# Late expert slots of an attention and mixture-of-experts kernel: rows gathered in quarters and turned on VectorE instead of TensorE

## The chip, the cores and the metric

One core of one Trainium2 chip runs the whole program. The metric is the device time of one execution in microseconds (us); for several executions it is their median. PE is TensorE's matmul, PEld its weight load, DVE is VectorE, ACT is ScalarE, POOL is GpSimd, SP is SyncE.

## The reference

The first half is an attention through 32 memory slots per head (8 batches, 8 heads, 576 rows, head width 64); its result, 4608 tokens of 512 numbers, is the input `x` of a mixture of 8 experts. Each token goes to the one expert with the largest logit:

```python
logits = x @ w_gate
e_idx = np.argmax(logits, axis=1)
...
for e in range(E):
    mask = e_idx == e
    h = np.maximum(x[mask] @ w1[e], 0.0)     # 512 -> 1024
    ye = h @ w2[e]                           # 1024 -> 512
    out[mask] = gate_w[mask, None] * eom[mask, e, None] * ye
```

The weights and the matmuls are float32. The kernel splits each operand into a rounded part and a rest (`xh`, `xl`; the two halves of `whl`; `hh`, `hl`) and adds three products.

## The kernel before

**Slots.** The experts' work is cut into slots of 3, 2 or 1 blocks of 128 tokens; all blocks of a slot belong to one expert, which is known only at run time. Slots 0 to 4 (three blocks each, index tables "a" and "b") are filled while attention still runs. Slots 5 to 9 (three blocks) and 10 to 13 (two blocks) are listed by the last table, "l", once all tokens are routed. Slots 14 and up hold one block each, stand behind branches and are not entered with these inputs, so the program works through 14 slots with 38 blocks.

**One slot** (`several`, L1111 to L1154). Its first layer takes four weight chunks of 128x1024 (u = 0 to 3) and runs 96 matmuls at L1127, weights standing, tokens moving; `hh` and `hl` come out of PSUM through ACT (L1132) and DVE (L1133). The second layer takes four chunks more (u = 4 to 7). For each chunk it goes through the slot's blocks k, and for each block it runs 6 matmuls at L1146 into the block's PSUM bank `py[k]`. One such group of 6 is a step: 12 steps in a slot of three blocks, 8 in one of two. Behind the last chunk of a block `finish_y` scales the block on ACT (L1106) and scatters its rows to `out` with an indirect DMA from POOL (L1107). Consecutive scatters write the same tensor, and each waits for the landing of the one before.

**Input of the next slot.** `gather` (L479 to L486) issues one indirect DMA on POOL per block, which brings one row of 576 floats per partition into `xg`; a row is four quarters of 144 floats, each 128 columns of `x` and 16 of gate numbers. The hook in the work loop issues the gathers of slot i+2 during slot i, behind the last scatter of slot i-1. At four fixed steps of slot i's second layer (`TURN`, `nxt`) `turn_x` (L978 to L995) turns the next slot's `xg`: TensorE transposes 128x128 squares against `ident` into a PSUM bank (L993), ACT copies the bank rounded to `xh` (L994), DVE subtracts that from the bank to `xl` (L995). Slots of three blocks do 3 transposes at each of the four steps; slots of two do 4 transposes at two of them. That is 4 transposes per block, 152 in all.

**Weights.** `Stream` fetches chunks from `wall` (512 KB each, SP queue), ACT casts (L521) and DVE subtracts (L522), up to 9 chunks ahead of use in a ring of 10.

**Index tables.** `table` (L205 to L242) builds an index list by 36 matmuls (L227), reads them from PSUM on DVE (L233 to L242) and writes `idx_g` for the gathers and `idx_o` for the scatters.

Of the kernel before, what the change touches and what calls it, by code (L numbers as in the profile page):

```python
# [16 lines left out]
P = 128  # L17
# [48 lines left out]
def attention_moe(tc, phiT, kv, qT, wgo, wall, out):  # L66
# [3 lines left out]
    with contextlib.ExitStack() as ctx:  # L70
# [20 lines left out]

        idx = {}
        for nm, n in (("a", 3 * NPS[0]), ("b", 3 * NPS[1]), ("l", NBL)):
            idx[nm] = (cp.tile([P, n], I32, name="idx_g" + nm), cp.tile([P, n], I32, name="idx_o" + nm))
# [46 lines left out]
        V.tensor_copy(tok_hl[:, 0], tok_j[:])  # L141
        V.tensor_scalar(tok_j[:], tiv, 63, None, ALU.bitwise_and)
        V.tensor_copy(tok_hl[:, 1], tok_j[:])
        su.__exit__(None, None, None)

        upto = cp.tile([P, E, E], F32, name="upto")
# [58 lines left out]
        def table(nm, q, nch, nblk):  # L205

            while nm == "l" and "rl" not in env:
                yield
            bw = (env["rl"] if nm == "l" else rt).tile([P, nch, 2, nblk], BF16, name="bw" + nm)
            w = min(nch, 9 * NBL // nblk // 9 * 9)  # L210
            for c in range(0, nch, w):
                b3 = [P, w, nblk]
                eq = rt.tile([P, 9 * NBL], BF16, name="eq")
                eq = eq[:, 0:w * nblk].rearrange("p (c b) -> p c b", c=w)
                V.tensor_tensor(eq, iota_blk[:, 0:nblk].unsqueeze(1).to_broadcast(b3),
                                q[:, c:c + w].unsqueeze(2).to_broadcast(b3), ALU.is_equal)
                yield
                for i in range(2):
                    V.tensor_tensor(bw[:, c:c + w, i], eq,
                                    tok_hl[:, i, c:c + w].unsqueeze(2).to_broadcast(b3), ALU.mult)  # L220
                yield
            yield
            yield from take_pr()
            yield from hold(LATE["pe"])
            pi = ps_r.tile([P, 2, NBL], F32, name="pr")
            for c in range(nch):
                T.matmul(pi[:, :, 0:nblk], Aw[:, c], bw[:, c], start=(c == 0), stop=(c == nch - 1))  # L227
            yield
            yield from hold(LATE["dve"])
            iv = rt.tile([P, NBL], F32, name="iv")  # L230
            i2 = rt.tile([P, NBL], F32, name="i2")
            ivv, i2v = iv[:, 0:nblk], i2[:, 0:nblk]
            V.tensor_copy(i2v, pi[:, 1, 0:nblk])  # L233
            yield
            V.scalar_tensor_tensor(ivv, pi[:, 0, 0:nblk], 64.0, i2v, ALU.mult, ALU.add)
            taken.clear()
            yield
            ig, io = idx[nm]
# [3 lines left out]
            V.scalar_tensor_tensor(io[:], ivv, -1.0, i2v, ALU.add, ALU.add)  # L242

        def counts(bp):
            pr = ps_r.tile([P, NCH, E], F32, name="pr")
# [60 lines left out]
        def route_late():  # L306
# [159 lines left out]
        for s in range(NSLOT):  # L466
            nb = 3 if s < NPE + NPT else 2 if s < NPE + NPT + NPP else 1
            if s < NPE:
                k = s >= NPS[0]
                nm, q0, rows = "ab"[k], 3 * (s - NPS[0] * k), (k + 2) * NCH * P  # L470
            else:
                j = s - NPE
                q0 = 3 * j if nb == 3 else NB3 + 2 * (j - NPT) if nb == 2 else NB3 + NB2 + j - NPT - NPP
                nm, rows = "l", NTOK
            slots.append({"s": s, "nb": nb, "q0": q0, "idx": idx[nm], "rows": rows,
                          "known": False, "listed": False})
        order = slots

        def gather(z):  # L479
            z["xg"] = xgs.tile()  # L480
            for k in range(z["nb"]):
                q = z["q0"] + k
                G.indirect_dma_start(  # L483
                    out=z["xg"][:, k], out_offset=None, in_=xs[0:z["rows"]],
                    in_offset=bass.IndirectOffsetOnAxis(ap=z["idx"][0][:, q:q + 1], axis=0),
                    bounds_check=z["rows"] - 1, oob_is_err=False)  # L486

        def known(*zs):
            for z in zs:
                z["known"] = True  # L490

        class Stream:
# [485 lines left out]
        def turn_x(z, c):  # L978


            nb, xg = z["nb"], z["xg"]
            if c == 0:
                z["x"] = (mo.tile([P, 4, 3 * P], F32R, name="xh"), mo.tile([P, 4, 3 * P], F32R, name="xl"))
            xh, xl = z["x"]
            n = nb * P
            w = 1 if nb == 3 else 2
            if c % w:
                return
            pt = bank([w, 512 // w], "ps")
            for j in range(w):  # L990
                for k in range(nb):
                    o = (c + j) * XQ
                    T.transpose(pt[:, j, k * P:(k + 1) * P], xg[:, k, o:o + P], ident[:])  # L993
            A.copy(xh[:, c:c + w, 0:n], pt[:, :, 0:n])  # L994
            V.tensor_tensor(xl[:, c:c + w, 0:n], pt[:, :, 0:n], xh[:, c:c + w, 0:n].bitcast(F32), ALU.subtract)  # L995

        NT = 5 * NBP
        deferred = []
# [104 lines left out]

        def finish_y(z, k, py):
            y = mo.tile([P, DM], F32, name="y", bufs=2)
            A.activation(y[:], py, AF.Copy, scale=z["xg"][:, k, P:P + 1])  # L1106
            G.indirect_dma_start(  # L1107
                out=out, out_offset=bass.IndirectOffsetOnAxis(ap=z["idx"][1][:, z["q0"] + k:z["q0"] + k + 1], axis=0),
                in_=y[:], in_offset=None, bounds_check=NTOK - 1, oob_is_err=False)

        def several(i, st, nxt, hook):  # L1111
# [29 lines left out]
            for u in range(4, 8):  # L1141
                w = st.take(i, u)
                for k in range(nb):
                    for f in range(2):
                        for n, (a, b) in enumerate(PASS):
                            T.matmul(py[k], h[u - 4][a][:, f, k * P:(k + 1) * P], w[:, b, DM * f:DM * f + DM],  # L1146
                                     start=(u == 4 and f == 0 and n == 0), stop=(u == 7 and f == 1 and n == 2))
                    if u == 7:
                        finish_y(z, k, py[k])
                    hook()  # L1150
                    step = nb * (u - 4) + k
                    if step in TURN[nb]:
                        nxt(TURN[nb].index(step))
                st.done(PUMP[0])  # L1154

        def single(i, st, nxt):
            z = order[i]
# [48 lines left out]
        def settle():  # L1206

            att.finish()
            pso.close()
            pa.close()  # L1210
            env["hs"] = ctx.enter_context(tc.tile_pool(name="hs", bufs=1, side="right", reuse_waits="tile"))
            env["rl"] = ctx.enter_context(tc.tile_pool(name="rl", bufs=1, side="right", reuse_waits="tile"))
            grow(1)
            env["ps"] = ctx.enter_context(tc.tile_pool(name="p1", bufs=7 - NPK, space=PSUM, reuse_waits="tile"))

# [49 lines left out]
def _layout(inputs):  # L1265
# [19 lines left out]
    wall = np.concatenate([w1, w2], axis=2)  # L1285
    return [("phiT", phiT), ("kv", kv), ("qT", qT), ("wgo", wgo), ("wall", wall)]


# [16 lines left out]
```

## Time and profile before

| | |
|---|---|
| median of 3 runs | 595.18 us (593.45 to 597.05) |
| the profiled execution, its own time | 595.97 us |
| span from first to last instruction in it | 594.3 us |
| PE busy | 539.3 us, 91% of the span |
| DVE, ACT, POOL busy | 340.9, 273.0, 160.7 us |
| matmuls | 4107 |

A row of the instruction timeline gives start and duration in us, the engine, line, operation and tiles, how many instructions are merged into it (x3), and in brackets how long the engine was idle before and who released it. Matmuls are pipelined: a matmul's duration overlaps the next ones, so what one costs is read from the distance between starts.

### The profile page before, as it was taken

Reading aid. Unit: us, or ns where it says so; the run is one execution under the profiler, and the core shown is the slowest. Engines: PE = TensorE matmul, PEld = TensorE weight load, DVE = VectorE, ACT = ScalarE, POOL = GpSimd, SP = SyncE. Lnnn points to the kernel's source line nnn. Section 1 sums busy time; section 2 is a strip of 40 time slices with the busy share of each in tenths; the row PEclk is TensorE's granted clock in tenths of the full one; section 3 lists DMA queues with packets and bytes.
Section 4 is the critical chain, followed back from the end, with each engine's and each line's share of the span. In section 5 each row is a group of like instructions: output and inputs, shape, how many; then the busy total and the mean of one; then the engine's idle time right before and its main releaser. Section 6 shows DMA issues by size and latency. Waiting matters only on the chain. (4 is left out here: it accounts for less than half of the span.)

```text
span 594.3 us, 10781 instructions
## 1 busy us (share of the span) xinstructions
PE 539.3 (91%) x4107; PEld 464.3 (78%) x4107; DVE 340.9 (57%) x686; ACT 273.0 (46%) x456; POOL 160.7 (27%) x192
## 2 busy tenths in 40 slices
PE   3788677788999999999999999999999999999980
PEld 2455455487788898998989899898989988989970
DVE  4487789677855589983544535354453526556200
ACT  4376554544445365434435444444444445555310
POOL 2244376731345036203303030130303012300100
PEclk9979879879999999999999999999999999999995
DMA  8999999974558578646646446474645538762000
GB/s 300 413 374 387 410 378 324 318 251 142 160 169 299 174 243 281 213 128 200 219 142 206 130 162 192 136 221 142 199 126 166 164 136 261 242 206 82 28 18 13
DMA packets 41276, 124.13 MB, mean 209 GB/s; under 512 B 9408, under 2 KB 9472, under 8 KB 40832
## 3 DMA queue, kind: packets, MB, share of 16 engines
q1 hardware_dynamic: 35136, 102.71, 52.2%
q0 software_dynamic: 6080, 20.65, 9.7%
q8 instruction: 34, 0.56, 0.4%
q14 instruction: 26, 0.21, 0.1%
HBM read 102.99 MB, written 20.87 MB: 208 GB/s over the span
## 5 line engine op out<-in xcount | busy, mean ns | idle before, releaser
L1127 PE MATMUL bps<-xh,whl 128*128 128x384 f32 (+1 forms) x896 | 213.8, 322 | 0.0
L1146 PE MATMUL bps<-whl,hh 128*128 128x512 f32 x608 | 203.7, 399 | 0.0
L522 DVE TENSOR_TENSOR whl<-w,whl 128x1024 fp32r<-128x1024 f32 x112 | 136.4, 1227 | 71.3 <-ACT whl L521 70.8
L1127 PEld LDWEIGHTS bps<-xh,whl 128*128 128x128 f32 x896 | 157.1, 190 | 1.4 <-issue 0.6
L1127 PE MATMUL bps<-xl,whl 128*128 128x384 f32 (+1 forms) x448 | 143.8, 321 | 0.0
L1146 PEld LDWEIGHTS bps<-whl,hh 128*128 128x128 f32 x608 | 114.2, 188 | 25.7 <-issue 2.5
L1146 PE MATMUL bps<-whl,hl 128*128 128x512 f32 x304 | 118.7, 390 | 0.0
L521 ACT CAST whl<-w 128x1024 fp32r<-128x1024 f32 x112 | 115.9, 1046 | 0.0
L1132 ACT ACTIVATE hh<-bps 128x384 fp32r<-128x384 f32 (+1 forms) x96 | 48.9, 510 | 102.0 <-PE bps L1127 97.7
L1133 DVE SCALAR_TENSOR_TENSOR hl<-bps,hh 128x384 fp32r<-128x384 f32 (+1 forms) x96 | 55.2, 576 | 58.9 <-ACT hh L1132 51.3
L1127 PEld LDWEIGHTS bps<-xl,whl 128*128 128x128 f32 x448 | 85.1, 190 | 0.5
L1107 POOL DMA_INDIRECT out<-y,idx_ol x23 | 23.1, 1003 | 213.7 <-ACT y L1106 186.4
L1146 PEld LDWEIGHTS bps<-whl,hl 128*128 128x128 f32 x304 | 57.3, 189 | 10.1
L995 DVE TENSOR_TENSOR xl<-bps,xh 128x384 fp32r<-128x384 f32 (+1 forms) x48 | 27.8, 579 | 60.7 <-ACT xh L994 60.5
L1106 ACT ACTIVATE y<-bps,xg 128x512 f32<-128x512 f32 x38 | 26.2, 689 | 68.9 <-issue 23.1
L994 ACT CAST xh<-bps 128x384 fp32r<-128x384 f32 (+1 forms) x48 | 23.9, 498 | 72.9 <-PE bps L993 71.2
L483 POOL DMA_INDIRECT xg<-xs,idx_gl x23 | 28.2, 1227 | 24.3 <-DVE idx_ol L242 17.6
L830 ACT COPY xo<-bpd 128x576 f32<-128x576 f32 x36 | 22.5, 639 | 22.5 <-PE bpd L828 13.1
L795 POOL TENSOR_TENSOR ea<-ea,mx 128x512 f32<-128x512 f32 (+1 forms) x20 | 19.2, 962 | 46.0 <-DVE mx L793 41.7
L828 PE MATMUL bpd<-ve_b,aT 64*128 64x144 f32 (+1 forms) x320 | 28.6, 327 | 2.1 <-DVE ea L790 1.9
L913 POOL TENSOR_SCALAR Aw<-iota_row,row 128x128 bf16<-128x128 bf16 x36 | 26.9, 763 | 12.4 <-DVE row L903 12.4
L993 PE MATMUL bps<-ident,xg 128*128 128x128 f32 x152 | 26.0, 286 | 2.3 <-DVE ea L790 1.8
(232 smaller groups left out, 427.1 us busy)
## 6 DMA issues: line engine op xcount, KB each, us to landing
w<-wall SPq DMA_DIRECT2D x112, 512.0 KB
kvt<-kv SPq DMA_DIRECT2D x32, 512.0 KB
xs<-xo SPq DMA_DIRECT2D x16, 576.0 KB
qt<-qT SPq DMA_DIRECT2D x16, 512.0 KB
ph<-phiT SPq DMA_DIRECT2D x3, 1152.0 KB
kv<-kv SPq DMA_DIRECT2D x4, 512.0 KB
ph<-phiT SPq DMA_DIRECT2D x4, 288.0 KB
xs<-xo SPq DMA_DIRECT2D x8, 144.0 KB
```

Source lines behind the costliest of these rows:

```text
L483: G.indirect_dma_start(out=z["xg"][:, k], out_offset=None, in_=xs[0:z["rows"]], in_offset=bass.IndirectOffsetOnAxis(ap=z["idx"][0][:, q:q ...
L521: A.copy(hl[:, 0], w[:])
L522: V.tensor_tensor(hl[:, 1], w[:], hl[:, 0].bitcast(F32), ALU.subtract)
L828: T.matmul(px[to:to + n, r, sl], z["aT"][h, o:o + n], ves[2 * bp + b][h, g], start=True, stop=True)
L913: (G if AWP else V).tensor_scalar(Aw[:, bp * NCH + c], iota_row[:], row[:, c:c + 1], None, ALU.is_equal)
L993: T.transpose(pt[:, j, k * P:(k + 1) * P], xg[:, k, o:o + P], ident[:])
L995: V.tensor_tensor(xl[:, c:c + w, 0:n], pt[:, :, 0:n], xh[:, c:c + w, 0:n].bitcast(F32), ALU.subtract)
L1106: A.activation(y[:], py, AF.Copy, scale=z["xg"][:, k, P:P + 1])
L1127: T.matmul(pb[:, j % pb.shape[1], 0:n_], w[:, b, o:o + P], x[a][:, cc, 0:n_], start=(n == 0), stop=(n == 11))
L1132: A.activation(h_[:, js, 0:n_], pb[:, :, 0:n_], AF.Relu)
L1133: V.scalar_tensor_tensor(l_[:, js, 0:n_], pb[:, :, 0:n_], 0.0, h_[:, js, 0:n_].bitcast(F32), ALU.max, ALU.subtract)
L1146: T.matmul(py[k], h[u - 4][a][:, f, k * P:(k + 1) * P], w[:, b, DM * f:DM * f + DM], start=(u == 4 and f == 0 and n == 0), stop=(u == 7 an ...
```

## The change

Slots from 6 on (`WHOLE` holds 0 to 5) are treated in another way.

- `gather` issues four indirect DMAs per block instead of one, each of which brings a quarter of a row (144 floats) to a partition: 80 gathers for the 20 blocks of slots 6 to 13 instead of 20. Partition 32a+i of column group b then holds quarter a of token 32b+i.
- `turn_x` has DVE transpose all 32x32 squares of 128 columns per block in one instruction per step (`xt`, in SBUF), and `xh` and `xl` are made from `xt`. There is one such instruction at each of the four steps for slots of two blocks too. The gate number of a token then lies in partitions 0 to 31; ACT puts it in place with four small copies per slot (`gx`).
- The contraction order of `x` differs with this, so a third set of chunks in `wall` holds `w1` in the new order, and chunks 0 to 3 of these slots are fetched from it.
- The quarter indices come from four more matmuls (`rep`) and five DVE instructions behind the table "l"; a column `quad` is made at the program's start (one iota on POOL, two DVE instructions), and `rep` by four DVE copies behind slot 1.
- The late slots' experts are declared known before the table "l" instead of behind it, so their weights may be fetched earlier.
- In the last slot (13) the second layer goes block by block instead of chunk by chunk.

```diff
+WHOLE = tuple(range(NPE + 1))
...
+            if nm != "l":
+                return
+            for z in order:
+                if z["nm"] == nm and not z["quart"]:
+                    z["listed"] = True
+
+            rep = env["rep"]
+            pq = ps_r.tile([P, 4, 2, NBL], F32, name="pr")
+            for b in range(4):
+                T.matmul(pq[:, b, :, 0:nblk], rep[:, b], hlv, start=True, stop=True)
...
+            V.tensor_scalar(iq[:], t4v, 4.0, quad[:, 0:1], ALU.mult, ALU.add)
...
+            known(*order[NPE:])
             yield from table("l", q1, NCHT, NBL)
-            known(*order[NPE:])
...
+                if z["quart"]:
+                    rows = 4 * z["rows"]
+                    for b in range(4):
+                        G.indirect_dma_start(
+                            out=z["xg"][:, k, XQ * b:XQ * b + XQ], out_offset=None,
+                            in_=xs[0:z["rows"]].rearrange("t (a q) -> (t a) q", a=4),
+                            in_offset=bass.IndirectOffsetOnAxis(ap=z["idx"][2][:, b, q:q + 1], axis=0),
+                            bounds_check=rows - 1, oob_is_err=False)
+                    continue
...
-                    nc.sync.dma_start(w[:], wall[bass.ds(z["e"], 1), :, self.fetched % 8])
+                    u = self.fetched % 8
+                    nc.sync.dma_start(w[:], wall[bass.ds(z["e"], 1), :, u + 8 * (z["quart"] and u < 4)])
...
+                if z["quart"]:
+                    z["g"] = env["xt"].tile([P, 3], F32, name="gx")
+                    for b in range(4):
+                        A.copy(z["g"][32 * b:32 * b + 32, 0:nb], xg[0:32, 0:nb, XQ * b + P])
             xh, xl = z["x"]
...
+            if z["quart"]:
+                xt = env["xt"].tile([P, 3 * P], F32, name="xt")
+                V.transpose(xt[:, 0:n].rearrange("p (k i) -> p k i", i=32),
+                            xg[:, 0:nb].rearrange("p k (b q) -> p (k b) q", b=4)[:, :, 32 * c:32 * c + 32])
+                pt = xt[:, 0:n]
+            else:
+                pt = bank([512], "ps")
                 for k in range(nb):
...
+            A.copy(xh[:, c, 0:n], pt)
+            V.tensor_tensor(xl[:, c, 0:n], pt, xh[:, c, 0:n].bitcast(F32), ALU.subtract)
...
+            turns = [(u, k) for u in range(4, 8) for k in range(nb)]
+            if 8 * i + 8 == st.hi:
+                turns.sort(key=lambda t: t[1])
+            for step, (u, k) in enumerate(turns):
...
+    w3 = inputs["moe_w1"][:, xhs].reshape(E, 4, 4, 32, 4, 256).transpose(0, 1, 3, 4, 2, 5).reshape(E, P, 4, 1024)
+    wall = np.concatenate([w1, w2, w3], axis=2)
```

Three places in the built programs show what moves. The numbers behind the names tell tiles of one name apart.

PE, before, in slot 5's second layer around the first step at which slot 6 is turned (`xg_3615` is slot 6's gathered input, `bps_3900` and `bps_3901` are the banks of blocks 1 and 2):

```order
L1146 MATMUL bps_3900<-whl_3524,hl_3743 128x512
L1146 MATMUL bps_3900<-whl_3524,hh_3742 128x512
L993 MATMUL bps_3916<-ident_61,xg_3615 128x128 x3
L1146 MATMUL bps_3901<-whl_3524,hh_3742 128x512
L1146 MATMUL bps_3901<-whl_3524,hl_3743 128x512
```

PE, now, at the same place (`bps_4284` and `bps_4285` are the same two banks):

```order
L1198 MATMUL bps_4284<-whl_3948,hl_4127 128x512
L1198 MATMUL bps_4284<-whl_3948,hh_4126 128x512
L1198 MATMUL bps_4285<-whl_3948,hh_4126 128x512
L1198 MATMUL bps_4285<-whl_3948,hl_4127 128x512
L1198 MATMUL bps_4285<-whl_3948,hh_4126 128x512 x2
```

The three transposes are gone, and the second layer's matmuls stand behind one another.

DVE, before, while slot 6 is turned:

```order
L522 TENSOR_TENSOR whl_3894<-w_3657,whl_3894 128x1024
L995 TENSOR_TENSOR xl_3915<-bps_3916,xh_3914 128x384
L522 TENSOR_TENSOR whl_3928<-w_3686,whl_3928 128x1024
L995 TENSOR_TENSOR xl_3915<-bps_3945,xh_3914 128x384
L522 TENSOR_TENSOR whl_3957<-w_3730,whl_3957 128x1024
L995 TENSOR_TENSOR xl_3915<-bps_3968,xh_3914 128x384
```

DVE, now, at the same place:

```order
L565 TENSOR_TENSOR whl_4278<-w_4014,whl_4278 128x1024
L1035 STREAM_TRANSPOSE xt_4305<-xg_3759 128x384
L1044 TENSOR_TENSOR xl_4299<-xt_4305,xh_4298 128x384
L565 TENSOR_TENSOR whl_4315<-w_4043,whl_4315 128x1024
L1035 STREAM_TRANSPOSE xt_4332<-xg_3759 128x384
L1044 TENSOR_TENSOR xl_4299<-xt_4332,xh_4298 128x384
L565 TENSOR_TENSOR whl_4342<-w_4087,whl_4342 128x1024
```

A transpose stands ahead of each `xl`, and `xl` reads `xt` in SBUF instead of a PSUM bank.

PE, before, at the end of the last slot's second layer (`bps_6361` is block 0's bank, `bps_6362` block 1's, `whl_6220` the last chunk):

```order
L1146 MATMUL bps_6361<-whl_6220,hh_6332 128x512
L1146 MATMUL bps_6361<-whl_6220,hl_6333 128x512
L1146 MATMUL bps_6361<-whl_6220,hh_6332 128x512 x2
L1146 MATMUL bps_6361<-whl_6220,hl_6333 128x512
L1146 MATMUL bps_6361<-whl_6220,hh_6332 128x512
L1146 MATMUL bps_6362<-whl_6220,hh_6332 128x512
```

PE, now, where block 0 ends in the last slot (`bps_6584` is block 0's bank, `bps_6585` block 1's, `whl_6443` the last chunk and `whl_6373` the first of the layer):

```order
L1198 MATMUL bps_6584<-whl_6443,hh_6555 128x512
L1198 MATMUL bps_6584<-whl_6443,hl_6556 128x512
L1198 MATMUL bps_6584<-whl_6443,hh_6555 128x512 x2
L1198 MATMUL bps_6584<-whl_6443,hl_6556 128x512
L1198 MATMUL bps_6584<-whl_6443,hh_6555 128x512
L1198 MATMUL bps_6585<-whl_6373,hh_6468 128x512
```

Before, 6 matmuls of block 1 follow block 0's last; now block 0 is complete after 24 of the layer's 48 matmuls, and 24 of block 1 follow.

More of the change, by code (lines that the diff above doesn't have):

```diff
@@ L93, in attention_moe @@
         for nm, n in (("a", 3 * NPS[0]), ("b", 3 * NPS[1]), ("l", NBL)):
-            idx[nm] = (cp.tile([P, n], I32, name="idx_g" + nm), cp.tile([P, n], I32, name="idx_o" + nm))
+            idx[nm] = (cp.tile([P, n], I32, name="idx_g" + nm), cp.tile([P, n], I32, name="idx_o" + nm),
+                       cp.tile([P, 4, n], I32, name="idx_q" + nm) if nm == "l" else None)
         slot = cp.tile([P, NSLOT + 1], I32, name="slot")
@@ L143, in attention_moe @@
         V.tensor_copy(tok_hl[:, 1], tok_j[:])
+        quad_i = ini.tile([P, 1], I32, name="quad_i")
+        G.iota(quad_i[:], pattern=[[1, 1]], base=0, channel_multiplier=1)
+        V.tensor_scalar(quad_i[:], quad_i[:], 5, None, ALU.arith_shift_right)
+        quad = cp.tile([P, 1], F32, name="quad")
+        V.tensor_copy(quad[:], quad_i[:])
         su.__exit__(None, None, None)
@@ L229, in table @@
             yield from hold(LATE["dve"])
+            hl = rt.tile([P, 2, NBL], BF16, name="hl_i")
             iv = rt.tile([P, NBL], F32, name="iv")
             i2 = rt.tile([P, NBL], F32, name="i2")
-            ivv, i2v = iv[:, 0:nblk], i2[:, 0:nblk]
-            V.tensor_copy(i2v, pi[:, 1, 0:nblk])
+            ivv, i2v, hlv = iv[:, 0:nblk], i2[:, 0:nblk], hl[:, :, 0:nblk]
+            V.tensor_copy(hlv, pi[:, :, 0:nblk])
             yield
-            V.scalar_tensor_tensor(ivv, pi[:, 0, 0:nblk], 64.0, i2v, ALU.mult, ALU.add)
-            taken.clear()
+            V.scalar_tensor_tensor(ivv, hlv[:, 0], 64.0, hlv[:, 1], ALU.mult, ALU.add)
+            if nm != "l":
+                taken.clear()
             yield
-            ig, io = idx[nm]
+            ig, io, iq = idx[nm]
             V.tensor_scalar(ig[:], ivv, 1.0, 0.0, ALU.subtract, ALU.max)
@@ L242, in table @@
             V.scalar_tensor_tensor(io[:], ivv, -1.0, i2v, ALU.add, ALU.add)
+            if nm != "l":
+                return
[6 more added lines that the diff above has]
+                T.matmul(pq[:, b, :, 0:nblk], rep[:, b], hlv, start=True, stop=True)
+            yield
+            yield from hold(LATE["dve"])
+            t4 = env["rl"].tile([P, 4, NBL], F32, name="iq")
+            t4v = t4[:, :, 0:nblk]
+            V.tensor_copy(t4v, pq[:, :, 1, 0:nblk])
+            yield
+            V.scalar_tensor_tensor(t4v, pq[:, :, 0, 0:nblk], 64.0, t4v, ALU.mult, ALU.add)
+            taken.clear()
+            yield
+            V.tensor_scalar(t4v, t4v, 1.0, 0.0, ALU.subtract, ALU.max)
+            yield
+            V.tensor_scalar(iq[:], t4v, 4.0, quad[:, 0:1], ALU.mult, ALU.add)
         def counts(bp):
@@ L475, in attention_moe @@
             slots.append({"s": s, "nb": nb, "q0": q0, "idx": idx[nm], "rows": rows,
+                          "nm": nm, "quart": s not in WHOLE,
                           "known": False, "listed": False})
@@ L981, in turn_x @@
             nb, xg = z["nb"], z["xg"]
+            n = nb * P
             if c == 0:
                 z["x"] = (mo.tile([P, 4, 3 * P], F32R, name="xh"), mo.tile([P, 4, 3 * P], F32R, name="xl"))
+                if z["quart"]:
+                    z["g"] = env["xt"].tile([P, 3], F32, name="gx")
+                    for b in range(4):
+                        A.copy(z["g"][32 * b:32 * b + 32, 0:nb], xg[0:32, 0:nb, XQ * b + P])
             xh, xl = z["x"]
[L985 to L990, printed above, removed]
+            if z["quart"]:
[5 more added lines that the diff above has]
+                pt = bank([512], "ps")
                 for k in range(nb):
[L992 to L995, printed above, removed]
+                    T.transpose(pt[:, k * P:(k + 1) * P], xg[:, k, c * XQ:c * XQ + P], ident[:])
+                pt = pt[:, 0:n]
+            A.copy(xh[:, c, 0:n], pt)
+            V.tensor_tensor(xl[:, c, 0:n], pt, xh[:, c, 0:n].bitcast(F32), ALU.subtract)
         NT = 5 * NBP
@@ L1105, in finish_y @@
             y = mo.tile([P, DM], F32, name="y", bufs=2)
-            A.activation(y[:], py, AF.Copy, scale=z["xg"][:, k, P:P + 1])
+            A.activation(y[:], py, AF.Copy, scale=z["g"][:, k:k + 1] if z["quart"] else z["xg"][:, k, P:P + 1])
             G.indirect_dma_start(
@@ L1140, in several @@
             py = [bank([DM], "ps") for _ in range(nb)]
-            for u in range(4, 8):
+            turns = [(u, k) for u in range(4, 8) for k in range(nb)]
+            if 8 * i + 8 == st.hi:
+                turns.sort(key=lambda t: t[1])
+            for step, (u, k) in enumerate(turns):
                 w = st.take(i, u)
[L1143 to L1154, printed above, removed]
+                for f in range(2):
+                    for n, (a, b) in enumerate(PASS):
+                        T.matmul(py[k], h[u - 4][a][:, f, k * P:(k + 1) * P], w[:, b, DM * f:DM * f + DM],
+                                 start=(u == 4 and f == 0 and n == 0), stop=(u == 7 and f == 1 and n == 2))
+                if u == 7:
+                    finish_y(z, k, py[k])
+                hook()
+                if step in TURN[nb]:
+                    nxt(TURN[nb].index(step))
+                if k == nb - 1:
+                    st.done(PUMP[0])
         def single(i, st, nxt):
@@ L1212, in settle @@
             env["rl"] = ctx.enter_context(tc.tile_pool(name="rl", bufs=1, side="right", reuse_waits="tile"))
+            env["xt"] = ctx.enter_context(tc.tile_pool(name="xt", bufs=2, side="right", reuse_waits="tile"))
+            env["rep"] = env["rl"].tile([P, 4, P], BF16, name="rep")
+            i4 = ident[:].rearrange("p (b i) -> p b i", b=4)
+            for b in range(4):
+                V.tensor_copy(env["rep"][:, b].rearrange("p (a i) -> p a i", a=4),
+                              i4[:, b:b + 1].to_broadcast([P, 4, 32]))
             grow(1)
@@ L1284, in _layout @@
     w2 = inputs["moe_w2"].reshape(E, 4, 2, P, DM).transpose(0, 3, 1, 2, 4).reshape(E, P, 4, 1024)
-    wall = np.concatenate([w1, w2], axis=2)
+    w3 = inputs["moe_w1"][:, xhs].reshape(E, 4, 4, 32, 4, 256).transpose(0, 1, 3, 4, 2, 5).reshape(E, P, 4, 1024)
+    wall = np.concatenate([w1, w2, w3], axis=2)
     return [("phiT", phiT), ("kv", kv), ("qT", qT), ("wgo", wgo), ("wall", wall)]
```

## The prediction, on record before the changed kernel ran

> **What bounds the kernel now.** I read the page first, then busy time by windows, then the timelines of PE, POOL and ACT around one turn of the next slot's input and at the end. The page's first lines and three windows (start:end, length, busy us of PE, PEld, DVE, ACT and POOL with counts, then granted clock, DMA share, GB/s): a slot of three blocks, one of two, and what follows the last matmul.
>
> ```profile
> span 594.3 us, 10781 instructions
> PE 539.3 (91%) x4107; PEld 464.3 (78%) x4107; DVE 340.9 (57%) x686; ACT 273.0 (46%) x456; POOL 160.7 (27%) x192
> ...
> 353.00:388.00 35.00, 35.00 (x185) 31.79 (x184) 16.48 (x21) 15.37 (x24) 6.03 (x6) 1.00 0.55 173
> 512.00:536.00 24.00, 24.00 (x160) 21.93 (x159) 14.48 (x15) 13.09 (x17) 4.76 (x5) 1.00 0.71 219
> 582.00:594.00 12.00, 0.00 (x0) 0.00 (x0) 0.00 (x0) 0.00 (x0) 0.76 (x1) 0.50 0.03 12
> ```
>
> PE has no gap in the late slots, at a granted clock of 1.00; DVE and ACT are busy for half of the time. So the late slots take as long as PE's own instruction stream, and a PE instruction that goes away there is time saved, while work added to DVE, ACT or POOL costs nothing until it makes PE wait. After the last matmul there are some 17 us (577.5 to 594.3) in which only scatters and the program's end run: there a chain of waits decides, not PE.
>
> **The transposes that leave PE.** 80 of 152 go (20 blocks of slots 6 to 13, four each). The group of all 152 gives them this busy time:
>
> ```profile
> L993 PE MATMUL bps<-ident,xg 128*128 128x128 f32 x152 | 26.0, 286 | 2.3 <-DVE ea L790 1.8 <-DMA xg<-xs,idx_ga 0.5
> ```
>
> That would be 80 x 0.286 = 22.9 us. But durations overlap, so the price is in the starts. One step's three transposes in a slot of three blocks, then four of them in a slot of two:
>
> ```profile
> 405.25 0.39 PE L1146 MATMUL bps<-whl,hl 128*128 128x512 f32 x1
> 405.48 0.39 PE L1146 MATMUL bps<-whl,hh 128*128 128x512 f32 x1
> 405.71 0.49 PE L993 MATMUL bps<-ident,xg 128*128 128x128 f32 x3
> 405.95 0.48 PE L1146 MATMUL bps<-whl,hh 128*128 128x512 f32 x1
> 406.27 0.39 PE L1146 MATMUL bps<-whl,hl 128*128 128x512 f32 x1
> ...
> 522.29 0.40 PE L1146 MATMUL bps<-whl,hh 128*128 128x512 f32 x1
> 522.53 0.60 PE L993 MATMUL bps<-ident,xg 128*128 128x128 f32 x4
> 522.88 0.48 PE L1146 MATMUL bps<-whl,hh 128*128 128x512 f32 x1
> 523.20 0.39 PE L1146 MATMUL bps<-whl,hl 128*128 128x512 f32 x1
> ```
>
> A matmul of 512 columns follows the last one after 0.23 us (405.25 to 405.48). From the matmul ahead of the transposes to the second behind them are 0.79 us (405.48 to 406.27) instead of 2 x 0.23: three transposes cost 0.33 us. Four cost 0.91 - 0.46 = 0.45 us. Slots 6 to 9 have four such places each, slots 10 to 13 two: 16 x 0.33 + 8 x 0.45 = 5.3 + 3.6 = 8.9 us. The slots' own periods check this, from scatter rows of POOL (the first scatters of slots 5, 6, 11, 12 and 13, and the last of 5 and 13):
>
> ```profile
> 345.43 1.02 POOL L1107 DMA_INDIRECT out<-y,idx_ol  x1 [22.03 <-ACT y L1106]
> ...
> 352.58 0.97 POOL L1107 DMA_INDIRECT out<-y,idx_ol  x1 [2.55 <-ACT hh L1132]
> ...
> 379.96 1.02 POOL L1107 DMA_INDIRECT out<-y,idx_ol  x1 [22.03 <-ACT y L1106]
> ...
> 531.49 1.02 POOL L1107 DMA_INDIRECT out<-y,idx_ol  x1 [15.13 <-ACT y L1106]
> ...
> 554.86 0.97 POOL L1107 DMA_INDIRECT out<-y,idx_ol  x1 [18.01 <-ACT y L1106]
> ...
> 577.28 0.97 POOL L1107 DMA_INDIRECT out<-y,idx_ol  x1 [17.93 <-ACT y L1106]
> 581.79 0.97 POOL L1107 DMA_INDIRECT out<-y,idx_ol  x1 [3.54 <-ACTq L1257]
> ```
>
> Slot 13 turns nothing for a successor: its period is 22.42 us (554.86 to 577.28) against 23.37 for slot 12 (531.49 to 554.86), 0.95 us for the eight transposes that 2 x 0.45 gives as 0.90. I take -9.0 us, bounds -8.7 to -9.4.
>
> The Trainium skill, page "VectorE: DVE Perf Modes", section "The three transpose paths", puts a 128x128 bf16 transpose on TensorE at 390 ns, and the rules behind it keep whole 128x128 squares on TensorE; by that figure 80 would be worth 31 us. No run here shows bf16; the f32 rows disagree with it as a price on the path, and the measurement decides.
>
> **What takes their place, and its cover.** Per slot of three blocks DVE gets four transposes in SBUF. The nearest rows, beside those of `y`, `xl`, `xh` and of the weights' rest:
>
> ```profile
> L522 DVE TENSOR_TENSOR whl<-w,whl 128x1024 fp32r<-128x1024 f32 x112 | 136.4, 1227 | 71.3 <-ACT whl L521 70.8 <-issue 0.4
> ...
> L1106 ACT ACTIVATE y<-bps,xg 128x512 f32<-128x512 f32 x38 | 26.2, 689 | 68.9 <-issue 23.1 <-PE bps L1146 21.8 <-DMA out<-y,idx_ol 8.0
> ...
> L995 DVE TENSOR_TENSOR xl<-bps,xh 128x384 fp32r<-128x384 f32 x40 | 22.2, 556 | 48.9 <-ACT xh L994 48.7
> ...
> L994 ACT CAST xh<-bps 128x384 fp32r<-128x384 f32 x40 | 19.2, 480 | 55.2 <-PE bps L993 53.5 <-issue 1.7
> ...
> L815 DVE STREAM_TRANSPOSE aT<-ea 128x512 f32<-128x512 f32 x16 | 10.8, 676 | 0.0
> ...
> L815 DVE STREAM_TRANSPOSE aT<-ea 128x256 f32<-128x256 f32 x4 | 1.6, 398 | 0.0
> ...
> L888 ACT ACTIVATE zs<-zs 128x9 f32<-128x9 f32 x4 | 0.8, 208 | 0.3 <-DVE zs L873 0.3
> ```
>
> Between 0.398 and 0.676 lies about 0.54 us for 384 columns: 2.2 us per slot on a DVE with 18.5 idle of 35 (first window). Slots of two blocks: 4 x 0.40 = 1.6 us with 9.5 idle of 24. ACT gets four small copies of about 0.21 us per slot, 0.8 us of 19.6 idle. All this is hidden as long as it is ready in time. The last step's `xh` comes behind the first block's `y` on ACT, as now, and no longer waits for PE: `y`, `xh`, `xl` are about 0.69 + 0.48 + 0.56 = 1.7 us after the first block's end, while PE still has two blocks' 12 matmuls, 2.8 us, and first needs this quarter of `x` only after three others. The cover is over 1 us; if it went, each lost us would cost 1 us in each of 8 slots.
>
> POOL gets 12 gathers instead of 3 per slot of three blocks, 8 instead of 2 for two. Rows of the gathers, and the DVE instruction beside the longer one:
>
> ```profile
> 391.85 1.23 DVE L522 TENSOR_TENSOR whl<-w,whl 128x1024 fp32r<-128x1024 f32 x1 [0.38 <-ACT whl L521]
> ...
> 391.95 2.01 POOL L483 DMA_INDIRECT xg<-xs,idx_gl  x1 [0.31 <-issue]
> 394.26 1.00 POOL L483 DMA_INDIRECT xg<-xs,idx_gl  x1 [0.30 <-issue]
> ```
>
> A gather takes 1.00 us alone, 2.01 where it starts beside L522, and 0.3 us lie between two. L522 runs 8 x 1.23 = 9.8 of 34.5 us, so about 0.28 of the gathers meet it: a mean of about 1.3, and 12 x 1.6 = 19 us. They are queued behind the last scatter of a slot and ahead of the first scatter of the next; between these POOL idles for 22.0 + 3 gathers x 1.3 = 26 us. So the scatters behind them aren't late, nor the `y` that waits for a scatter's landing. The new gathers have to be ready a whole slot later, so their landing costs 0; the waiting instruction would be DVE's first transpose, with the weights' rest queued behind it, 9 chunks ahead of PE. More packets of a quarter of the size on DMA queues that are 0.55 to 0.71 busy: 0.
>
> **Small adds.** The four index matmuls: the nearest row is the table's 36.
>
> ```profile
> 261.63 1.68 PE L227 MATMUL pr<-bwl,Aw 128*128 128x90 bf16 x36
> 263.15 0.51 PE L993 MATMUL bps<-ident,xg 128*128 128x128 f32 x3
> ```
>
> 1.52 us for 36 is 0.04 each: +0.2 us, if DVE's copy that they wait for is early enough; bounds 0 to +1. Weights known earlier, and the third set of chunks: PE waits for no weights now, so 0. The column at the start lies ahead of the first softmax, which DVE starts right behind its setup:
>
> ```profile
> 6.13 0.11 DVE L147 MEMSET upto<- 128x64 f32 x1
> 6.16 2.69 DVE L634 TENSOR_REDUCE nmx<-ph 128x1 f32<-128x576 f32 x4
> ```
>
> Two DVE instructions of about 0.2 us (the 208 ns row) delay it by 0.4, which the loads behind it may swallow: +0.2, bounds 0 to +0.4.
>
> **The end.** Block 0 of the last slot is complete 18 matmuls earlier (42nd to 24th of 48), 18 x 0.23 = 4.1 us. The two last `y` on ACT, and the chain of waits around the scatters:
>
> ```profile
> 576.32 0.69 ACT L1106 ACTIVATE y<-bps,xg 128x512 f32<-128x512 f32 x1 [9.00 <-PE bps L1146]
> 577.68 0.69 ACT L1106 ACTIVATE y<-bps,xg 128x512 f32<-128x512 f32 x1 [0.67 <-PEq L1257]
> ...
> 577.28 3.74 DMA out<-y,idx_ol
> ...
> 581.06 0.52 issue
> ```
>
> Now the last scatter starts at 581.79, 0.77 us after the first has landed (577.28 + 3.74 = 581.02), though its `y` was ready at 577.68 + 0.69 = 578.37. With block 0 earlier, the first scatter starts at 573.2 and lands at 576.9, ahead of that `y`. Then the last scatter follows its `y`, as the first does, 0.27 us behind (576.32 + 0.69 = 577.01 to 577.28): 578.64, or 579.14 if the 0.77 stays. The saving is 3.15 or 2.65; I take -2.9. All that follows hangs on that scatter and moves with it.
>
> **Sum.** -9.0 + 0.2 + 0.2 - 2.9 = -11.5 us, from 595.97 us (span 594.3 and what lies around it) to 584.5. That execution lies 0.8 us above the median of 595.18, from which the same gives 583.7. I forecast 584.0.
>
> **Rivals.** *POOL becomes the bound (slower).* If a quarter gather cost more than a row's, POOL would need per slot of three blocks 12 x (g + 0.3) and, from first to last scatter, 352.58 - 345.43 + 1.3 = 8.4 us, against 34.53 - 1.3 = 33.2 us of PE. From g = 1.77 us POOL falls behind; over the four slots (4 to 7) that issue 12 gathers by 4 x (12g - 21.2). Scatters then come late, ACT stands at a `y` whose buffer a scatter holds, and PE fills its free banks and stops; I put that at 6 us of lag (three free banks of the eight that a first layer of half of 33.2 us fills), so it decides from g = 1.9. At g = 2.5 the lag is 35 us, 29 lost against 11.5 gained: 613 us. For it: the 2.01 row. Against it: the 1.00 row, and that a gather addresses 128 pieces either way. 5 in 100. The Trainium skill, "SBUF — State Buffer", section "Who interferes with whom", says that a DVE instruction with two SBUF inputs and a GpSimd instruction that reads SBUF exclude each other for a whole instruction. The trace agrees in the 2.01 row; by the rule `xl` now joins L522, since both its inputs lie in SBUF. That adds 4 x 0.56 to L522's 9.8 of 34.5 us, so 0.35 of the gathers meet one: g about 1.35.
>
> *PE waits for the new chain (transpose, `xh`, `xl`).* The cover of over 1 us goes and each of 8 slots loses about 0.7 us: 590. For it: three in-order queues hand over per step. Against it: nothing in the chain waits for PE any more. 11 in 100.
>
> *The end doesn't move,* because something else orders the last scatter: 584.5 + 2.9 = 587.4. 5 in 100. *The transposes are worth their busy time:* 595.2 - 22.9 - 2.9 + 0.4 = 570. The starts speak against it. 2 in 100.
>
> **Numbers.** That leaves 77 in 100 for the forecast. The known bounds alone give 582.9 to 585.4 from the median; a run's own spread of 0.3% and most of the second and third rival widen it to 581.0 to 589.0, and about 2 in 10 stay outside. A difference of 0.5% (3.0 us) is about what a measurement of this kernel can tell from none. Faster by more: 0.92 (all but the first rival and a fifth of the second); within: 0.03; slower: 0.05.
>
> **What would show it.** In the profile after, the slots of three blocks from the sixth on should have a period of 33.2 us and those of two 22.4, PE without a gap, the 512-column matmuls 0.23 us apart where the transposes stood. Gathers should have a mean near 1.3 us and POOL an idle stretch ahead of each slot's first scatter; the last scatter should start about 1 us behind the last matmul. Wrong would be: gaps on PE ahead of a slot's first matmul, a gather mean near 2 us, or first scatters of a slot that wait for no `y`.

## The result, and the profile after

The changed kernel takes 579.6 us (median of 4 runs, 577.36 to 580.24), the kernel before in the same comparison 594.58 (4 runs): a ratio of 0.9736, interval 0.9694 to 0.9777. It is faster, by 15.0 us where 11.5 were forecast, and its median lies 1.4 us below the lower end of the range. The profiled execution after is the fastest of the four, 577.36 us, with a span of 575.6.

The page of the changed kernel: the span, the engines' busy times, then the groups of the new gathers (busy us, mean ns of one, idle before), of `xh` and of `xl`.

```profile
span 575.6 us, 10886 instructions
...
PE 529.1 (92%) x4031; PEld 455.6 (79%) x4031; DVE 356.1 (62%) x736; ACT 280.4 (49%) x496; POOL 229.2 (40%) x253
...
L519 POOL DMA_INDIRECT xg<-xs,idx_ql x80 | 90.2, 1127 | 25.2 <-issue 24.3
...
L1043 ACT CAST xh<-xt 128x384 fp32r<-128x384 f32 (+1 forms) x32 | 14.7, 460 | 37.9 <-DVE xt L1035 37.9
...
L1044 DVE TENSOR_TENSOR xl<-xt,xh 128x384 fp32r<-128x384 f32 (+1 forms) x32 | 15.8, 492 | 24.1 <-ACT xh L1043 24.1
```

PE has 76 matmuls fewer (80 transposes less 4 index matmuls) and 10.2 us less busy time. The gathers cost POOL 90 us, and a gather's mean is 1.127 us, not 1.3. The same windows as before, for a slot of three blocks and one of two:

```profile
353.00:388.00 35.00, 35.00 (x181) 32.15 (x181) 18.68 (x25) 17.51 (x29) 17.85 (x17) 1.00 0.61 182
512.00:536.00 24.00, 24.00 (x153) 21.83 (x152) 16.86 (x22) 14.81 (x27) 9.87 (x9) 1.00 0.66 199
```

PE still has no gap, while DVE, ACT and POOL have more work and room left. So the late slots are still as long as PE's own stream. PE's timeline gives what a slot saves: the first matmul of slots 6 and 7 before, then after.

```profile
347.32 0.33 PE L1127 MATMUL bps<-xh,whl 128*128 128x384 f32 x1
...
381.84 0.33 PE L1127 MATMUL bps<-xh,whl 128*128 128x384 f32 x1
```

```profile
345.01 0.33 PE L1176 MATMUL bps<-xh,whl 128*128 128x384 f32 x1
...
378.04 0.33 PE L1176 MATMUL bps<-xh,whl 128*128 128x384 f32 x1
```

34.52 us have become 33.03: 1.50 us per slot that turned a slot of three blocks (its first layer stays at 16.67 us, its second goes from 17.87 to 16.36). Slots 9 to 12 save 0.95 each, and slot 13, which turns nothing for a successor, saves nothing.

The end, on POOL and ACT, in the changed kernel: the two last `y` and their scatters.

```profile
561.61 0.69 ACT L1155 ACTIVATE y<-bps,gx 128x512 f32<-128x512 f32 x1 [4.86 <-PE bps L1198]
562.57 0.97 POOL L1156 DMA_INDIRECT out<-y,idx_ol  x1 [11.44 <-ACT y L1155]
567.04 0.69 ACT L1155 ACTIVATE y<-bps,gx 128x512 f32<-128x512 f32 x1 [4.75 <-PEq L1316]
568.01 0.97 POOL L1156 DMA_INDIRECT out<-y,idx_ol  x1 [4.47 <-ACT y L1155]
```

The last scatter starts 1.44 us behind the start of the last matmul (566.57); before it was 4.59 (581.79 against 577.20). Behind it something changed that no step of the prediction had. The instructions of the program's end on POOL's sequencer (POOLq), by line: duration min/median/max in ns and when they start. Before:

```profile
L1257 POOLq INC_SWDGE_SEM  x1: 1708/1708/1708, 585.4 to 585.4; - x1
...
L1301 POOLq DRAIN  x3: 45/107/6284, 587.1 to 594.0; - x3
```

After:

```profile
L1316 POOLq INC_SWDGE_SEM  x1: 795/795/795, 571.4 to 571.4; - x1
...
L1362 POOLq DRAIN  x3: 45/107/2530, 572.3 to 575.4; - x3
```

One INC_SWDGE_SEM and one long DRAIN stand between the last scatter's landing and the end (these are the profile's names; what the two do is not in the trace). They took 8.0 us together before and 3.3 after. From the last scatter's start to the end of the span are 594.3 - 581.79 = 12.5 us before and 575.6 - 568.01 = 7.6 after. I call this stretch the end stretch.

The spans differ by 18.7 us: 0.8 up to slot 4's first matmul (278.26 and 277.48), 9.85 from there to the last matmul, 3.15 up to the last scatter and 4.9 in the end stretch. That is more than the 15.0 between the medians, because the execution profiled after is the fastest of its four.

### The profile page after: what moved, and what is told of

The parts are those of the page before. It is cut to its first block, busy times and chain, and to the rows that moved or that the text cites. A ratio compares the mean times of both kernels' runs of the same rounds, so it can differ in the third digit from the quotient of the medians.

```text
span 575.6 us, 10886 instructions
## 1 busy us (share of the span) xinstructions
PE 529.1 (92%) x4031; PEld 455.6 (79%) x4031; DVE 356.1 (62%) x736; ACT 280.4 (49%) x496; POOL 229.2 (40%) x253
## 3 DMA queue, kind: packets, MB, share of 16 engines
q0 software_dynamic: 7040, 20.65, 10.4%
## 5 line engine op out<-in xcount | busy, mean ns | idle before, releaser
L1198 PE MATMUL bps<-whl,hh 128*128 128x512 f32 x608 | 197.7, 396 | 0.0
L519 POOL DMA_INDIRECT xg<-xs,idx_ql x80 | 90.2, 1127 | 25.2 <-issue 24.3
L1156 POOL DMA_INDIRECT out<-y,idx_ol x23 | 24.9, 1081 | 127.1 <-ACT y L1155 101.4
L1198 PEld LDWEIGHTS bps<-whl,hl 128*128 128x128 f32 x304 | 57.5, 189 | 10.8
L1043 ACT CAST xh<-xt 128x384 fp32r<-128x384 f32 (+1 forms) x32 | 14.7, 460 | 37.9 <-DVE xt L1035 37.9
L956 POOL TENSOR_SCALAR Aw<-iota_row,row 128x128 bf16<-128x128 bf16 x36 | 26.8, 759 | 12.4 <-DVE row L946 12.4
L1044 DVE TENSOR_TENSOR xl<-xt,xh 128x384 fp32r<-128x384 f32 (+1 forms) x32 | 15.8, 492 | 24.1 <-ACT xh L1043 24.1
L1155 ACT ACTIVATE y<-bps,gx 128x512 f32<-128x512 f32 x20 | 13.4, 687 | 30.4 <-PE bps L1198 13.9
L871 PEld LDWEIGHTS bpd<-ve_b,aT 64*128 64x128 f32 (+1 forms) x320 | 21.7, 196 | 8.1 <-issue 3.5
```

The source lines that it names most:

```text
L519: G.indirect_dma_start(out=z["xg"][:, k, XQ * b:XQ * b + XQ], out_offset=None, in_=xs[0:z["rows"]].rearrange("t (a q) -> (t a) q", a=4), i ...
L871: T.matmul(px[to:to + n, r, sl], z["aT"][h, o:o + n], ves[2 * bp + b][h, g], start=True, stop=True)
L956: (G if AWP else V).tensor_scalar(Aw[:, bp * NCH + c], iota_row[:], row[:, c:c + 1], None, ALU.is_equal)
L1156: G.indirect_dma_start(out=out, out_offset=bass.IndirectOffsetOnAxis(ap=z["idx"][1][:, z["q0"] + k:z["q0"] + k + 1], axis=0), in_=y[:], in ...
```

## The experiments

**Is the short end chance?** Theory A says that the forecast's terms are right and the end stretch varies by itself; theory B that the change shortens it. Four kernels: the two as they are, and each part alone. "last_only" is the kernel before with this edit, "quarters_only" the changed kernel without it:

```
-            for u in range(4, 8):
+            turns = [(u, k) for u in range(4, 8) for k in range(nb)]
+            if 8 * i + 8 == st.hi:
+                turns.sort(key=lambda t: t[1])
+            for step, (u, k) in enumerate(turns):
...
```

before_again: 

> The kernel before, unchanged, for the spread and for the length of the program's end. Theory A (the three parts of the change add up, the end's length is chance): ratio 1.000 within 0.004, and the stretch from the start of the last scatter to the end of the span, 12.5 us in the profile before, comes out anywhere between 7 and 13 us. Theory B (the change itself shortened that stretch to 7.6 us): ratio 1.000, and the stretch is 12 us or more again.

last_only: 

> The kernel before with only the last slot's second layer block by block. Theory A: the last scatter starts 1.4 us behind the last matmul's start instead of 4.6 us, so 3.1 us faster than before, ratio 0.9948. Theory B with the end's gain tied to this part: 3.1 + 4.9 = 8 us faster, ratio 0.9865. Rival that the end doesn't move: ratio 1.000.

quarters_only: 

> The changed kernel with the last slot's second layer in the old order, chunk by chunk. Theory A: only the transposes' 9.8 us are saved (period 33.0 us in slots of three blocks, 22.4 in slots of two), ratio 0.9835, and the last scatter starts 4.6 us behind the last matmul. Theory B with the end's gain tied to this part: 14.7 us faster, ratio 0.975.

after_again: 

> The changed kernel again. Theory A: 9.8 + 3.1 = 12.9 us faster, ratio 0.978, with the stretch behind the last scatter's start anywhere between 7 and 13 us. Theory B: 15 to 18 us faster, ratio 0.970 to 0.975, with that stretch at 7.6 us within 1 us.

Measured: before_again 595.08 (ratio 0.9998, 0.9976 to 1.0021), last_only 593.36 (0.9952, 0.9934 to 0.9969), quarters_only 581.85 (0.9760, 0.9734 to 0.9786), after_again 579.4 (0.9728, 0.9702 to 0.9754). The last scatters of last_only, on POOL (its last matmul starts at 576.36, its span is 590.3):

```profile
572.36 0.97 POOL L1107 DMA_INDIRECT out<-y,idx_ol  x1 [13.85 <-ACT y L1106]
577.87 0.97 POOL L1107 DMA_INDIRECT out<-y,idx_ol  x1 [4.55 <-ACT y L1106]
```

The order alone brings the last scatter to 1.5 us behind the last matmul and leaves the end stretch at 12.4. In quarters_only the last scatter comes 4.06 us behind and the end stretch is 7.7. In before_again and after_again the two instructions take 1708 and 6284, 795 and 2530 ns as in the first traces. Theory A falls: the short end comes with the quarters.

**What in the quarters shortens it, and what is a transpose worth?** Theory C: the number of indirect DMAs that POOL issues (76 before, 136 after). Theory D: the transposes, or the smaller pieces. no_turn takes the transposes away and leaves the DMAs as they are:

```
+            if z["s"] > 5:
+                px = xg[:, 0:nb, c * XQ:c * XQ + P]
+                hv, lv = (t[:, c, 0:n].rearrange("p (k i) -> p k i", i=P) for t in (xh, xl))
+                A.copy(hv, px)
+                V.tensor_tensor(lv, px, hv.bitcast(F32), ALU.subtract)
+                return
```

no_turn: 

> The kernel before, but the input of slots 6 to 13 is not turned at all: the rounded part and the rest are made straight from the gathered rows (this leaves out the turning, 80 transposes on PE and nothing in their place); rows are gathered as before, 76 indirect DMAs on POOL (38 gathers, 38 scatters). It measures what the transposes cost on the path. From the periods of the two traces the forecast is 9.8 us (1.50 for each of four slots of three blocks, 0.95 for each of four of two). Theory C (the program's end is shorter because POOL issues more indirect DMAs, 136 instead of 76): the end stays at 12.4 us behind the last scatter's start, about 585.3, ratio 0.9835. Theory D (it is shorter because the transposes leave PE, or the DMAs' pieces are smaller): if it hangs on the transposes, the end is 7.7 us, about 580.5, ratio 0.975. If the transposes were worth their busy time of 22.9 us: 572, ratio 0.96.

Measured: 585.17 (0.9829, 0.9806 to 0.9853), last scatter at 571.01, span 583.2, end stretch 12.2. PE at the first matmuls of slots 6 and 7:

```profile
344.36 0.33 PE L1133 MATMUL bps<-xh,whl 128*128 128x384 f32 x1
...
377.39 0.33 PE L1133 MATMUL bps<-xh,whl 128*128 128x384 f32 x1
```

33.03 us, as in the changed kernel: DVE's new work costs PE nothing, and the transposes are worth 9.8 us on the path. They are not what shortens the end.

more_gathers is the kernel before with useless gathers behind the real ones, 136 DMAs in all:

```
+                for _ in range(3 * (z["s"] > 5)):
+                    G.indirect_dma_start(
+                        out=env["xt"].tile([P, XQ], F32, name="spare", bufs=4)[:], out_offset=None,
+                        in_=xs[0:z["rows"]].rearrange("t (a q) -> (t a) q", a=4),
+                        in_offset=bass.IndirectOffsetOnAxis(ap=z["idx"][0][:, q:q + 1], axis=0),
+                        bounds_check=4 * z["rows"] - 1, oob_is_err=False)
...
```

more_gathers: 

> The kernel before, with three further indirect gathers of a quarter row behind each of the 20 row gathers of slots 6 to 13, into a spare tile that nobody reads: 136 indirect DMAs on POOL as in the changed kernel, and everything else as before. Theory C (more indirect DMAs on POOL make the program's end shorter): last scatter where it is in the kernel before, the end behind its start 7.7 us instead of 12.4, about 590.4, ratio 0.992. Theory D (transposes, order of instructions, or what PE does): 12.4 us, about 595, ratio 1.000. If POOL's extra work delayed the scatters: over 597, and PE with gaps.

Measured: 591.86 (0.9945, 0.9925 to 0.9966), faster than the kernel before although it only does more. The same two instructions:

```profile
L1264 POOLq INC_SWDGE_SEM  x1: 795/795/795, 589.5 to 589.5; - x1
...
L1308 POOLq DRAIN  x3: 45/107/2530, 590.3 to 593.4; - x3
```

These are the changed kernel's values to the nanosecond, with the transposes still on PE and the old order. The end stretch is 593.7 - 585.92 = 7.8 us. The time fell by 3.3 us (2.0 to 4.5) where 4.7 were expected. The end is as short as theory C has it, so something ahead of it took the rest; no run shows what. (The profiled execution, 595.42, is the longest of its 12; in it the matmuls at 404 to 408 us stand 0.72 us apart for "issue" while DVE and ACT idle, a pause of some 3 us whose cause I can't name.) Theory C holds so far.

pairs_only quarters slots 10 to 13 alone, 100 DMAs:

```
-WHOLE = tuple(range(NPE + 1))
+WHOLE = tuple(range(NPE + NPT))
```

pairs_only: 

> The changed kernel with the quarters only in slots 10 to 13 (two blocks each): 32 quarter gathers, 30 row gathers and 38 scatters, 100 indirect DMAs on POOL; the last slot block by block. By the periods, slots 9 to 12 save 0.95 us each, 3.8 us, and the last scatter comes 3.15 us earlier for the order: 6.95 us. If the end behind the last scatter's start stays at 12.4 us: about 588.1, ratio 0.988. If it is 7.7 us as with 136: about 583.4, ratio 0.980. If it shrinks by the number of DMAs (24 of 60 more): 10.5 us, about 586.2, ratio 0.985.

Measured: 592.38 (0.9947, 0.9926 to 0.9967), none of the three forecasts. Its last scatter starts at 574.85 and its span is 590.0: an end stretch of 15.1, longer than with 76.

```profile
L1316 POOLq INC_SWDGE_SEM  x1: 2188/2188/2188, 578.2 to 578.2; - x1
...
L1362 POOLq DRAIN  x3: 45/248/8247, 580.4 to 589.7; - x3
```

24 DMAs more cost 480 and 1963 ns, 20 and 82 ns each. So more DMAs lengthen the end, and somewhere between 100 and 136 it falls. That, with the 216 DMAs of gather_twice (below), gave theory C its second form: the end costs 0.102 us for each DMA still open, and at some point POOL settles about 106 of them at once. Theory F: the stretch shrinks in another way. more_36 and more_48 are more_gathers with one and with two useless gathers, instead of three, per block of slots 6 to 9.

more_36: 

> The kernel before with 36 further quarter gathers into a spare tile that nobody reads (one behind each row gather of slots 6 to 9, three behind each of slots 10 to 13): 112 indirect DMAs on POOL. The runs so far give the stretch from the last scatter's start to the program's end as 12.4 us with 76 such DMAs, 15.2 with 100, 7.7 with 136 and 16.0 with 216. Theory C, in a form made from these four: 4.7 us and 0.102 us for each DMA that has not been settled yet, and somewhere behind 110 open ones about 106 are settled at once while POOL works. Then 112 gives either 4.7 + 11.4 = 16.1 us (not settled yet) or 4.7 + 0.6 = 5.3 us (settled), nothing between. Theory F (the stretch shrinks with the number of DMAs in another way, by steps or by chance): something between 7.7 and 15 us.

more_48: 

> As the run with 36, but two further gathers behind each row gather of slots 6 to 9: 124 indirect DMAs on POOL. Theory C: either 4.7 + 12.6 = 17.3 us (not settled yet) or 4.7 + 18 x 0.102 = 6.5 us (106 settled) from the last scatter's start to the end; if the run with 112 was short, this one must be 1.2 us longer than it. Theory F: something between 7.7 and 15 us.

Measured, one execution each: 599.31 us with 112 DMAs, last scatter at 581.59, span 597.6, end stretch 16.0; and 587.96 us with 124, 579.73, 586.2 and 6.5. First more_36, then more_48:

```profile
L1264 POOLq INC_SWDGE_SEM  x1: 2428/2428/2428, 585.1 to 585.1; - x1
...
L1308 POOLq DRAIN  x3: 45/107/9224, 587.5 to 597.3; - x3
```

```profile
L1264 POOLq INC_SWDGE_SEM  x1: 548/548/548, 583.3 to 583.3; - x1
...
L1308 POOLq DRAIN  x3: 45/107/1550, 583.8 to 586.0; - x3
```

Theory C had 16.1 or 5.3 for the first, 17.3 or 6.5 for the second; the traces have 16.0 and 6.5. Twelve useless gathers make the end 9.5 us shorter. The queue's packets and bytes don't explain it: the page counts 7232 software packets for more_36 (long), and 7040 for the changed kernel and 7616 for more_48 (short).

**Is POOL a bound?** gather_twice is the changed kernel with a copy of L519's issue behind it, into a spare tile.

gather_twice: 

> The changed kernel with each quarter gather issued a second time into a spare tile that nobody reads: 24 instead of 12 gathers on POOL per slot of three blocks. The rival of the prediction (POOL becomes the bound): per such slot POOL needs 24 x 1.44 (busy 1.13 and 0.31 to the next) + 8.4 from first to last scatter = 43 us against PE's 33.0, a lag of 10 us per slot in slots 4 to 7, less about 6 us that free banks take up: about 32 us lost, 611 us, with PE gaps in the late slots and scatters that wait for nothing but POOL itself. If POOL has room for twice the gathers: 579.6 us as in the changed kernel, PE without gaps.

Measured: 642.51 us, 63 more than the changed kernel, where 32 were expected. POOL in slot 6, and the one group that PE waited for between 354 and 486 us (us in total, times, longest):

```profile
366.51 1.00 POOL L519 DMA_INDIRECT xg<-xs,idx_ql  x1 [0.30 <-issue]
367.82 0.99 POOL L525 DMA_INDIRECT spare<-xs,idx_ql  x1 [0.30 <-issue]
369.11 1.02 POOL L1162 DMA_INDIRECT out<-y,idx_ol  x1 [0.30 <-issue]
372.70 0.99 POOL L1162 DMA_INDIRECT out<-y,idx_ol  x1 [2.57 <-ACT y L1161]
```

```profile
PE bps L1182 <- ACT y L1161: 25.7, 3, 9.0
```

The first scatter (369.11) waits for nothing but POOL itself; PE stands for a bank that ACT's `y` has not emptied. That is the rival's mechanism as it was told. The gathers' mean is 1.20 us here, so POOL needs 24 x 1.50 + 8.4 = 44.4 us a slot, and slots 6 to 8 have periods of 43.4, 44.5 and 44.4. PE idles for 25.7 of the 33.3 us that these three lose; nearly all of the rest passes at a lower clock behind each wait. The granted clock is 1.00 from 363 to 365 us, 0.50 from 374 to 376 and again from 464 to 466, and the first 16 matmuls behind the first wait (372.74 to 377.97) take 5.2 us instead of the 2.8 that 16 of them take elsewhere. The span is 65.0 us longer than that of the changed kernel's trace: slots 4 to 8 lose 40.6 us, the slots of two blocks 13.5 (the expectation had no term for them), the end stretch 8.4 (16.0 us with 216 DMAs), and 2.0 lie ahead of slot 4. The mechanism was right, and the price too low: with slots 4 to 8 losing 40.6 us, the lag of four times 10 was paid in full and not less 6 for free banks, and two terms were left out.

**What is a transpose worth?** turn_twice issues each late transpose of the kernel before twice:

```
-                    T.transpose(pt[:, j, k * P:(k + 1) * P], xg[:, k, o:o + P], ident[:])
+                    for _ in range(1 + (z["s"] > 5)):
+                        T.transpose(pt[:, j, k * P:(k + 1) * P], xg[:, k, o:o + P], ident[:])
```

turn_twice: 

> The kernel before with each of the 80 late transposes on PE issued twice in a row. If the price of a transpose on the path is per instruction, as the prediction has it (0.33 us for three, 0.45 for four), the doubled ones cost 8.9 us again: about 604, ratio 1.015. If a part of the price is paid once for each change from matmuls to transposes and back (the slower matmuls behind it), the second copy costs less than 8.9 us; if the whole price were the change, nothing: 595. The end behind the last scatter stays at 12.4 us (76 indirect DMAs).

Measured: 603.76 (1.0143, 1.0104 to 1.0181), end stretch 12.4. The interval is too wide to tell 8.9 us from a little less, so the trace has to. One place on PE:

```profile
367.31 0.39 PE L1147 MATMUL bps<-whl,hh 128*128 128x512 f32 x1
367.54 0.82 PE L994 MATMUL bps<-ident,xg 128*128 128x128 f32 x6
368.11 0.48 PE L1147 MATMUL bps<-whl,hh 128*128 128x512 f32 x1
368.42 0.40 PE L1147 MATMUL bps<-whl,hl 128*128 128x512 f32 x1
```

From the matmul ahead to the second behind are 1.11 us, against 0.79 with three. A slot's period grows by 1.21 us for twelve copies (348.11 to 383.85, 35.74), while taking the twelve away saves 1.50. So about 0.10 us is paid per transpose and some 0.07 us once per place.

**A version with one slot more.** slot5_too sets `WHOLE` to `tuple(range(NPE))`.

slot5_too: 

> The changed kernel with slot 5 gathered in quarters as well (89 quarter gathers and fewer row gathers, 145 indirect DMAs on POOL). Slot 4's second layer loses its 12 transposes: -1.5 us; nine more DMAs to settle at the end: +0.9 us by theory C. Together about 579.0 against 579.6, ratio to the kernel before 0.973; without theory C's part 578.1. Against it: slot 5's gathers come right behind the last index table, twelve of them in place of three (17 us on POOL), and PE may wait for them at slot 5's first matmul; if they come late by more than slot 4's cover, some us slower than the changed kernel.

Measured: 579.5 us (0.9731, 0.9703 to 0.9759), not to be told from the changed kernel. Slot 4 falls to 33.02 us (-1.5), but slot 5 takes 33.83, 0.8 more, with the one gap on PE in its first layer:

```profile
325.07 0.34 PE L1176 MATMUL bps<-xh,whl 128*128 128x384 f32 x1
325.69 0.45 PE L1176 MATMUL bps<-xh,whl 128*128 128x384 f32 x1 [0.29 <-DVE hl L1182]
```

Its two end instructions take 975 and 3265 ns, together 0.9 us more than the changed kernel's, as nine DMAs should: the saving is spent. So of the kernels tried none is clearly better than the changed one.

## Why the prediction was right and where it failed

- **The transposes** (-9.0): right in kind, a little small: 9.8 in the changed kernel and in no_turn. I measured the price between the matmul ahead and the second behind, against 2 x 0.23. Matmuls farther behind a change stand some ns farther apart too, and a second layer without transposes runs at 16.36 / 72 = 0.2272 us a matmul. The price of 0.33 for three is the 0.30 that turn_twice shows for the transposes themselves and part of the change. The 390 ns that the Trainium skill's "VectorE: DVE Perf Modes", section "The three transpose paths", gives for a bf16 transpose on TensorE is no price on this path: turn_twice shows 0.10 us for an f32 one.
- **What takes their place** (0): right. PE has no gap, and no_turn, without DVE's transposes, has the same period. A transpose on DVE took 0.57 us for three blocks and 0.44 for two, against 0.54 and 0.40.
- **The small adds** (+0.4): too small, not settled. From slot 3's first matmul to slot 4's, where the index matmuls lie, are 36.27 us instead of 36.06, the forecast +0.2. But slot 4's first matmul starts at 276.31 to 279.21 us (mean 277.51) in the eight traces with row gathers and at 277.48 to 279.51 (mean 278.85) in the six with quarters: 1.3 us later, with about 0.5 of uncertainty. The other 1.1 lie ahead of slot 1 and were not taken apart. About half of that is in slot 0, whose length from its first matmul to slot 1's is 46.3 to 46.9 us in some traces of either kind and 47.4 to 47.7 in others (two of the eight, four of the six), so it may in part be chance.
- **The end** (-2.9): -3.15, a bound that was given. That the end doesn't move is refuted by last_only.
- **The bounds**: added from the median, the bounds of the terms give 582.6 to 585.2, not the 582.9 to 585.4 that the prediction has. The difference changes nothing: 579.6 lies below both.
- **The step that failed** is "All that follows hangs on that scatter and moves with it." It hangs on it, but its length isn't fixed: 12.5 us became 7.6. With the forecast's -9.0, +0.4 and -2.9 this -4.8 would have given -16.3. With the measured terms the sum is -9.8 + 1.3 - 3.15 - 4.8 = -16.4, inside the interval of after_again (595.1 x 0.0272 = 16.2, from 14.6 to 17.7).
- **The rivals.** POOL became the bound only with the number of gathers doubled (gather_twice). The condition had the right form, and in the changed kernel the gathers stayed at 1.13 us. They wait less than I put: the row of 2.01 us was close to the worst case (the longest gather of that trace takes 2.09), not the price of each meeting. The estimate of 1.35 from the rule in the Trainium skill's "SBUF — State Buffer", section "Who interferes with whom", is too high too: the group's mean here is 1.127. No wait of PE for the new chain is in the changed kernel's trace.

## What to carry to other kernels

Price an instruction that leaves a full engine by the starts of its neighbours over a whole loop, not over its own place, and by the period of a loop that lacks it. What follows the last instruction of the work is part of the time: look at its rows, ask what sets each, and treat it as fixed only after two kernels show it the same. A change that alters how many DMAs POOL issues can move the end by several us either way.

## What the runs showed of the hardware

The end stretch by the number of indirect DMAs on POOL (for 76 and 136 from the first two traces; the others with these numbers have the same two durations, and end stretches of 12.2 to 12.5 and 7.6 to 7.8):

| DMAs | 76 | 100 | 112 | 124 | 136 | 145 | 216 |
|---|---|---|---|---|---|---|---|
| INC_SWDGE_SEM, ns | 1708 | 2188 | 2428 | 548 | 795 | 975 | 2395 |
| long DRAIN, ns | 6284 | 8247 | 9224 | 1550 | 2530 | 3265 | 9063 |
| end stretch, us | 12.5 | 15.1 | 16.0 | 6.5 | 7.6 | 8.6 | 16.0 |

Both instructions grow by 20 and 82 ns per DMA from 76 to 112, and again from 124 to 216, shifted by 106 DMAs: 216 costs as much as 110 would. The numbers fit if about 106 are settled during the run, between the 113th and the 124th DMA and once in up to 216. No gather or scatter from the 113th to the 124th takes more than 2.03 us in these traces, while 106 DMAs cost 10.8 at the end, so if it happens there it is hidden or free. That the two instructions give back what the DMAs hold is my reading; the runs show only the dependence on the number. Each of these DMAs has 128 rows or quarters of rows, so the runs can't tell the number of DMAs from the number of pieces. The Trainium skill, "VectorE: DVE Perf Modes", section "The DRAIN you can't avoid", puts the DRAINs that the runtime adds around a kernel at a constant of about 12 ns on all engines. The DRAINs here carry a line of the kernel (its `TileContext`, L1301 before): on DVE, ACT and PE's sequencer they take 8 to 17 ns, but POOL's long one takes 1550 to 9224, so that figure is not to be carried over to it.
